# A fused Nystrom attention and squared-ReLU MLP on one core: every batch's steps on three engines follow a written list, and PSUM banks are given out by role

## The chip, the cores and the metric

The kernel runs on one core of a Trainium2 chip. The time is device microseconds of one execution, taken as the median of several. A core has five engines that run side by side, each with its own queue of instructions: TensorE (PE in the profile, with its weight loads as PEld), VectorE (DVE), ScalarE (ACT), GpSimd (POOL) and SyncE (SP). PE writes its results to PSUM, which has eight banks; DVE and ACT read them from there.

## The reference

```python
# q, k, v: 8 batches x 8 heads x 576 rows x 64; m = 32 landmarks
q_lm = q.reshape(B, H, m, S // m, D).mean(axis=3)      # segment means, the same for k
A, Bm, C = sm(q, k_lm), sm(q_lm, k_lm), sm(q_lm, k)    # softmax of 1/8 * a @ b.T
Z = Bm.T / (norm1(Bm) * norminf(Bm) + 1e-06)
for _ in range(6):
    Z = 2 * Z - Z @ Bm @ Z                             # an approximate inverse of Bm
x = (A @ Z @ C @ v)                                    # heads side by side: 4608 x 512
h = x @ w_in                                           # 512 x 2048
out = relu(h) ** 2 @ w_out                             # 2048 x 512, float32
```

## The kernel before

One batch at a time goes through attention and then through the MLP. The attention output x of a batch is never formed. The kernel keeps the transposed A of a batch (the tile `AT`) and multiplies the small rest (Z, C, v) into `w_in`, which gives `G`. Then h is `G` times `AT`.

The attention of a batch is made of these steps, all in `attention`:

- `prepare` casts the loaded k or q (`raw`) to the layout that the matmuls want (`nat`, one DVE copy of 128x2048 each, L189). From batch 3 on (`DMA_T`) it also issues the DMA transposes from SP that make `T` from `nat` and `tT` from the 64 tail rows (L191, L197). Batches 0 to 2 are transposed by PE (`transposed`, L227) and copied out of PSUM by DVE and ACT. `nat` has one buffer for k and one for q, and the raw loads share two.
- `segment_means` (L254, L264), `landmark_scores` (L284) and `landmark_softmax` make the landmark matrix. `inverse_begin` and `inverse_first` prepare its inverse.
- The inverse is a chain: three `joint_step`, one `last_joint_step`, then two pairs of `b_times_v` and `newton_step`. Each is two small matmuls on PE (L326), one or two short DVE operations on their result (L331, L317), and then the next pair of matmuls, which needs what DVE wrote.
- `scores` (L409) and `tails` (L419) multiply `T` and `tT` with the landmarks, and ACT takes the exponential (L413, L421, L424). `a_quad_sums` and `a_rows` normalise A on DVE (L433, L445), `a_transposed` makes `AT` (L455), and `c_values` makes C times v (L477, L483).
- The last part folds: `wt` (L602), its copy (L609), and four groups of matmuls `g` (L627), whose results ACT and DVE copy to `G` in turn (L640 for the first and third, L642 for the second and fourth).

The MLP of a batch has 16 calls of `mlp_in` (four matmuls `h` at L656, a ReLU `r` on ACT at L663, a square to `gT` on DVE at L664) and its output tiles. `mlp_out` makes 16 matmuls for one tile of 128 rows (L686), then ACT copies the tile out of PSUM (`o_sb`, L695) and issues its DMA (L704). Two batches make nine tiles, because the 64 tail rows of both share one.

The work of neighbouring batches is interleaved. While batch b goes through `mlp_in`, batch b + 1 goes through attention, and output tiles of earlier work fill in. The call order comes from the loop at the end of the kernel: three or two output matmuls after each `mlp_in`, and a share of the attention's steps by `attend`. Only batch 0's opening is under `manual_schedule`, where an engine's instructions stand as the code emits them. For all else the framework's scheduler places the instructions of each engine, and some `issue_after` lines hold single ones back.

Loads of k, q and v are issued from POOL in one queue: at the start, `w_in` in four parts, v and k and q of batches 0 and 1, `w_out` in four parts, and then batch 2 and so on, each one when its buffer is free.

PSUM before: `h` has two buffers of two banks each (for `mlp_in`, for `g` and for some output tiles), the tag `n` has three buffers of one bank that everything else takes in turn, output tiles included, and `o` has one bank for the remaining output tiles.

Of the kernel before, what the change touches and what calls it, by code (L numbers as in the profile page):

```python
# [30 lines left out]
DMA_T = 3  # L31


@with_exitstack
def kernel(
# [134 lines left out]
    def ntile(shape, dt=F32):  # L170
        return psum.tile(shape, dt, tag="n", bufs=3, name="n")
# [39 lines left out]
    def attention(b: int, R: dict):  # L211
# [6 lines left out]
        def transposed(nm, half):  # L218
            if not first:
                tps = ntile([P, 2, NPAIR, P], BF16)[:]  # L220
            else:
                if half == 0:
                    X["tps"] = psum.tile([P, 4, NPAIR, P], BF16, tag="h", bufs=2, name="tps")
                tps = X["tps"][:, 2 * half:2 * half + 2, :, :]
# [9 lines left out]
        def transposed_tail():  # L234
            tps = ntile([P, NPAIR, P], BF16)
# [6 lines left out]
        means = ntile([P, 2, NPAIR, M])  # L242
# [36 lines left out]
        def landmark_scores():  # L279
            bm = ntile([P, 2, M])  # L280
# [39 lines left out]
        def products(diagonal, moving):  # L320
            n, w = moving(0).shape[-1], diagonal.shape[-1]
            res = ntile([P, 2, n])
# [11 lines left out]
        def inverse_begin():  # L334
# [3 lines left out]
            if first:  # L338
                rows = ntile([P, 2, M])
# [64 lines left out]
        def scores(nm, qd):  # L404
            sc = ntile([P, NC4, 2, 2, M])
# [10 lines left out]
        def tails():  # L416
            tl = ntile([P, NPAIR, 2, 2 * M])
# [32 lines left out]
        def a_transposed(i):  # L450
            tps = ntile([P, (NC4 + 1) * P], BF16)
# [13 lines left out]
        def c_values():  # L465

            cv = ntile([P, 2, D + 1])
# [67 lines left out]
        else:  # L535
            segment_means(1, "k")
            yield
            if b == 1:
                for half, evac in ((0, dve), (1, act)):
                    evac(*transposed("k", half))  # L540
                    yield
            segment_means(0, "q")
            yield
            landmark_scores()
            landmark_softmax()
            yield
            if b < DMA_T:
                dve(*transposed("q", 0))
            yield
            begun = inverse_begin()  # L550
            yield
            BT, ED = inverse_first(*begun)
            yield
            if b < DMA_T:
                act(*transposed("q", 1))
                yield
                if b > 1:
                    dve(*transposed("k", 0))
                    yield
                    act(*transposed("k", 1))  # L560
                    yield
                transposed_tail()
                yield
            side = [[(scores, "q", 0)], [(scores, "q", 1)], [(tails,)],
                    [(a_quad_sums, 0), (scores, "k", 0)], [(scores, "k", 1), (a_rows, 0)],
                    [(a_quad_sums, 1), (a_transposed, 0)], [(c_values,)],
                    [(a_rows, 1)], [(a_transposed, 1)]]

# [3 lines left out]

        if not first:
            aside()
            yield
        for it in range(3):
            EY, ED, last = joint_step(EY, ED)
            if it == 0 and b > 1:
                X["kpin"] = X["qpin"] = last
# [7 lines left out]
        for it in range(2):  # L587
# [6 lines left out]
            if it == 0 or not first:  # L594
                aside()
            yield
        zt = y.rearrange("p q a m -> p q (a m)")


        wt = ntile([P, 2, P])  # L600
        for qd in range(2):
            nc.tensor.matmul(wt[:, qd, :], lhsT=cvb.rearrange("p q d -> p (q d)"), rhs=zt[:, qd, :],  # L602
                             start=True, stop=True)
        WT = small.tile([P, 2, P], BF16, tag="WT", name="WT")
        if first:
            aside()
            nc.scalar.copy(WT[:], wt[:])
        else:
            last = nc.vector.tensor_copy(WT[:], wt[:])  # L609
        if b == 1:  # L610
            X["kpin"] = last
        if first:
            warm(2)
        yield


        for n in range(4):
            with in_turn() if first and n >= 2 else (
# [13 lines left out]
            if first:  # L632
                for c in ((0, 256), (256, 512)) if n == 0 else ((0, 512),):
                    if c[0]:
                        a_transposed(1)
# [162 lines left out]
```

## Time and profile before

| what | value |
|---|---|
| median of 4 runs | 269.95 us (269.52 to 270.41) |
| the profiled execution | 270.41 us, of which the span from first to last instruction is 268.6 us |
| instructions | PE 2793 matmuls, DVE 492, ACT 278, POOL 70 |
| matmuls of `mlp_in` (L656) and of `mlp_out` (L686) | 512 and 592 |

A page of the profile gives busy time by engine, then the chain of work that ended last, then groups of instructions by source line with busy time, the mean duration of one, and the idle time before them with what ended it. The timeline lists instructions by start time in us, then their length. Matmuls are pipelined: the length of one is from its start until its result is written, and the next one can start long before that. The distance from start to start is therefore what a matmul costs PE. The chip's clock for PE was granted in full throughout.

### The profile page before, as it was taken

Reading aid. Unit: us, or ns where it says so; the run is one execution under the profiler, and the core shown is the slowest. Engines: PE = TensorE matmul, PEld = TensorE weight load, DVE = VectorE, ACT = ScalarE, POOL = GpSimd, SP = SyncE. Lnnn points to the kernel's source line nnn. Section 1 sums busy time; section 2 is a strip of 40 time slices with the busy share of each in tenths; the row PEclk is TensorE's granted clock in tenths of the full one; section 3 lists DMA queues with packets and bytes.
Section 4 is the critical chain, followed back from the end, with each engine's and each line's share of the span. In section 5 each row is a group of like instructions: output and inputs, shape, how many; then the busy total and the mean of one; then the engine's idle time right before and its main releaser. Section 6 shows DMA issues by size and latency. Waiting matters only on the chain.

```text
span 268.6 us, 6785 instructions
## 1 busy us (share of the span) xinstructions
PE 252.2 (94%) x2793; PEld 149.4 (56%) x2793; DVE 175.8 (65%) x492; ACT 158.0 (59%) x278; POOL 46.2 (17%) x70
## 2 busy tenths in 40 slices
PE   2878899999999999999999999999999999999994
PEld 0745565467645665466555665466546665466443
DVE  4686878887965679458955778458945767454000
ACT  2367866369726774468736774478646673587110
POOL 8834333312220121021120132000000000000000
PEclk9999999999999999999999999999999999999999
DMA  8999999999899969992999979991811111210222
GB/s 183 181 205 196 206 203 190 226 189 142 97 162 207 148 124 158 136 180 45 149 171 180 104 133 167 125 158 57 181 41 39 41 39 41 78 43 15 63 81 78
DMA packets 69791, 34.65 MB, mean 129 GB/s; under 512 B 37376, under 2 KB 64256, under 8 KB 69760
## 3 DMA queue, kind: packets, MB, share of 16 engines
q0 software_dynamic: 39808, 17.83, 56.8%
q1 hardware_dynamic: 24704, 7.08, 20.4%
q10 hardware_dynamic: 5248, 9.31, 10.9%
q8 instruction: 22, 0.36, 0.5%
q14 instruction: 9, 0.07, 0.1%
HBM read 36.70 MB, written 9.44 MB: 172 GB/s over the span
## 4 chain that ended last, share of the span: by engine, by line
PE 72%; DVE 8%; ACT 7%; DMA 6%; issue 3%; POOL 2%; POOLq 0%; DVEq 0%; ACTq 0%
PE ops L686 34%; PE h L656 17%; PE n L686 7%; DMA w_out_bf<-in_moe_w_out_dram 6%; ACT G L640 3%; PE g L627 3%; ACT r L663 2%; PE n L254 2%; DVE ra L433 2%; PE n L326 2%; DVE gT L664 2%; PE n L409 2%; PE n L455 1%; PE n L477 1%; PE n L227 1%
## 5 line engine op out<-in xcount | busy, mean ns | idle before, releaser
L686 PE MATMUL ops<-w_out_bf,gT 128*128 128x512 bf16 (+1 forms) x480 | 119.5, 372 | 1.8 <-DMA w_out_bf<-in_moe_w_out_dram 1.3
L663 ACT ACTIVATE r<-h 128x576 bf16<-128x576 f32 x128 | 82.9, 658 | 27.1 <-PE h L656 22.8
L656 PE MATMUL h<-AT,G 128*128 128x288 bf16 x512 | 83.2, 285 | 1.8 <-ACT G L640 1.2
L664 DVE TENSOR_TENSOR gT<-r 128x576 bf16<-128x576 bf16 x128 | 58.0, 454 | 33.4 <-ACT r L663 32.5
L686 PEld LDWEIGHTS <-gT 128*128 128x128 bf16 x592 | 53.4, 97 | 39.9 <-issue 6.9
L656 PEld LDWEIGHTS <-G 128*128 128x128 bf16 x512 | 45.2, 97 | 21.6 <-issue 5.3
L695 ACT COPY o_sb<-ops 128x512 f32<-128x512 f32 (+1 forms) x29 | 16.7, 578 | 35.2 <-PE ops L686 35.2
L686 PE MATMUL n<-w_out_bf,gT 128*128 128x512 bf16 x112 | 31.9, 380 | 0.0
L642 DVE CAST G<-g 128x1024 bf16<-128x1024 f32 x14 | 17.1, 1225 | 13.0 <-PE g L627 12.9
L640 ACT CAST G<-g 128x1024 bf16<-128x1024 f32 x14 | 14.2, 1012 | 11.5 <-PE g L627 11.5
L409 PEld LDWEIGHTS <-T 128*128 128x128 bf16 x256 | 11.3, 98 | 5.4 <-issue 0.3
L326 PEld LDWEIGHTS <-ED 128*128 128x128 bf16 x84 | 7.2, 97 | 11.4 <-DVE ED L317 5.3
L445 DVE TENSOR_TENSOR an<-EA,rra 128x640 bf16<-128x640 f32 (+2 forms) x17 | 13.2, 779 | 0.2
L82 POOL DMA_DIRECT2D qkt<-in_k_dram x8 | 5.8, 720 | 43.9 <-PE n L264 29.3
L433 DVE TENSOR_REDUCE ra<-EA 128x20 f32<-128x640 f32 (+1 forms) x19 | 13.0, 701 | 0.4
L409 PE MATMUL n<-bd,T 128*128 128x64 bf16 x256 | 12.8, 193 | 0.0
L104 POOL DMA_DIRECT2D vm<-in_v_dram x8 | 7.1, 883 | 33.0 <-PE n L477 31.4
L459 ACT COPY AT<-n 128x576 bf16<-128x576 bf16 x9 | 5.8, 640 | 11.8 <-PE n L455 11.8
L94 POOL DMA_DIRECT2D raw<-in_k_dram x7 | 6.7, 959 | 29.5 <-DVE nat L189 18.8
L254 PEld LDWEIGHTS <-nat 128*128 128x128 bf16 x256 | 8.9, 97 | 5.0 <-DVE gT L664 1.4
L413 ACT ACTIVATE EA<-n 128x512 f32<-128x512 f32 x16 | 9.5, 600 | 2.2 <-PE n L409 2.1
L413 ACT ACTIVATE EC<-n 128x512 bf16<-128x512 f32 x16 | 9.6, 603 | 1.2 <-PE n L409 0.7
(125 smaller groups left out, 268.4 us busy)
## 6 DMA issues: line engine op xcount, KB each, us to landing
out_dram<-o_sb ACTq DMA_DIRECT2D x31, 256.0 KB, 4.3
vm<-in_v_dram POOLq DMA_DIRECT2D x8, 512.0 KB, 14.3
raw<-in_k_dram POOLq DMA_DIRECT2D x7, 512.0 KB, 10.3
raw<-in_q_dram POOLq DMA_DIRECT2D x7, 512.0 KB, 14.8
w_in_bf<-in_moe_w_in_dram POOLq DMA_DIRECT2D x4, 512.0 KB, 11.4
w_out_bf<-in_moe_w_out_dram POOLq DMA_DIRECT2D x4, 512.0 KB, 16.0
out_dram<-o_sb ACTq DMA_DIRECT2D x9, 128.0 KB, 2.4
raw<-in_k_dram SPq DMA_DIRECT2D x1, 1024.0 KB, 5.4
```

The costliest lines, as they stand in the source:

```text
L254: nc.tensor.matmul(means[:, ti, p, :], lhsT=src.rearrange("p h d -> p (h d)"), rhs=seg[:, c + (ti if c == NC4 else 0), :], start=(n == 0 a ...
L409: nc.tensor.matmul(sc[:, c, j, :, :], lhsT=X[nm + "T"][:, c, p, :], rhs=BD[:, 1 if nm == "q" else 0, p, 0:64], start=True, stop=True)
L413: nc.scalar.activation((EA if nm == "q" else EC)[:, qd, 0:NC4, :], sc.rearrange("p c j i m -> p c (j i m)"), AF.Exp, scale=SCALE)
L433: nc.vector.reduce_sum(ra[:, quads, lo:hi, :], EA[:, quads, lo:hi, :].rearrange("p q c (h m) -> p q c h m", m=M), axis=AX.X)
L445: nc.vector.tensor_tensor(an[:, i, lo:hi, :].rearrange("p c (h m) -> p c h m", m=M), EA[:, i, lo:hi, :].rearrange("p c (h m) -> p c h m", ...
L640: nc.scalar.copy(dst, gg[:])
L642: last = nc.vector.tensor_copy(dst, gg[:])
L656: last = nc.tensor.matmul(h[:, j, 0:HALF], lhsT=G[:, qd, f * P:(f + 1) * P], rhs=AT[:, qd, j * HALF:(j + 1) * HALF], start=(qd == 0), stop ...
L663: nc.scalar.activation(r.rearrange("p (j t) -> p j t", j=2), h[:, :, 0:HALF], AF.Relu)
L664: return nc.vector.tensor_tensor(gT[:, f, o:o + S], r[:], r[:], ALU.mult)
L686: mark[:] = [nc.tensor.matmul(ops, lhsT=gT[:, f, t * P:t * P + P], rhs=w_out_bf[:, f, i * n:i * n + n], start=(f == 0), stop=(f == NF - 1))]
L695: nc.scalar.copy(o_h, ops)
```

## The change

All batches now run under `manual_schedule` for PE, DVE and ACT, so that the instructions of each of these engines stand in the order in which the code emits them. That order is read from a list for each batch (`PLANS`): batch 0, batch 1, then one list for even and one for odd batches, and one for the last. POOL and SP are still placed by the scheduler.

In a list `h` is one `mlp_in` of batch b up to its ReLU, and `s` is the square of the oldest `h` that has none yet, so that DVE's square can stand apart from its ReLU. A number is so many matmuls of the output tiles. The other words are attention steps of batch b + 1: `mk` and `mq` are the segment means, `lm` and `ls` the landmark scores and their softmax, `ib` and `if` the start of the inverse, `jo` and `jl` the joint steps, `nu` and `nn` the later pairs, `sq0` to `sk1` the scores, `tl` the tails, `as` and `ar` the sums and rows of A, `at` its transposition, `cv` the C values, `wt` the fold, and `gg0` and `gg1` two of the four groups `g` each. `tk`, `tq` and `tt` are PE transposes, in the first two lists only. `pk` and `pq` are `prepare`, and a `+` means one batch further.

PSUM: `h` serves `mlp_in` and `g` alone. `n0` holds the attention's results, one at a time; `n1` holds the products of the inverse, the transposes of q, and the fold; `n2` and `o` take output tiles in turn. While batch 0's own attention runs, the three `n` banks are still taken in turn.

The output DMA of a tile is issued from ACT after the third matmul of the next tile instead of straight after its copy, other than in the last batch.

```diff
+PLACED = 1
+BATCH0 = (
+    "h h s s g h pk s h s h h g s h s h s tk0 h h s pq mk s h s h mq tq0 h s s 2 lm ls s h "
+    "tk1 ib tq1 1 h h 1 tt 1 if 2 s 1 sq0 1 jo s 2 sq1 jo s 1 tl jo 2 as0 3 sk1 jl 3 ar0 3 "
+    "sk0 2 as1 1 nu at0 2 ar1 nn pk+ 1 cv 1 nu nn1 1 at1 wt pq+ 2 gg0 2 gg1"
+)
+BATCH1 = (
+    "1 mk 1 h tq0 1 h mq h s tq1 2 lm h s 1 s h ls 1 tt s 1 s h ib sq0 h s 2 h tl 1 if 4 s "
+    "sq1 as0 2 jo h tk0 s 1 h jo 1 s tk1 1 pk+ 1 h jo s pq+ 1 sk0 1 as1 3 sk1 1 jl ar0 s h 1 "
+    "h ar1 cv 1 nu h 1 s h nn at0 3 nu 1 s 1 h nn1 3 s 1 wt at1 2 s 2 s 1 gg0 8 gg1 12"
+)
+EVEN = (
+    "2 h h 2 s s 1 mk mq 1 h 1 s 3 lm h ls 1 sq0 h 1 s 1 h 1 s ib 3 s tl h 2 if sq1 h as1 3 "
+    "jo sk0 h pk+ 2 s as0 2 s 2 jo s 1 h sk1 h 2 s h pq+ jo cv 2 jl s 1 ar0 2 h h 1 s nu 1 "
+    "ar1 2 h nn s 1 s h at0 s 3 nu 3 at1 1 nn1 4 wt s 4 gg0 5 gg1 7"
+)
+ODD = (
+    "2 h s mk 1 h 1 h mq 1 h 2 lm 1 s ls 1 s h s 4 s sq0 1 ib h 1 s tl if 2 h 1 sq1 h pk+ 1 "
+    "jo s as0 s 1 h 1 sk0 2 s 1 h 1 sk1 jo 1 s 1 h as1 h jo s pq+ 1 cv jl 4 h s ar0 1 nu h "
+    "ar1 3 s 1 nn h 3 s at0 h 1 nu at1 1 s 1 nn1 3 s 3 wt 4 gg0 8 gg1 15"
+)
+LAST = (
+    "1 h h 1 s 4 h 1 s s h 1 h 2 s 1 h 1 s 6 s 1 h s h 3 h s 2 h 1 s 2 s 1 h 2 s 3 h 2 s h h "
+    "1 s 3 h 4 h 7 s s s"
+)
+PLANS = [BATCH0, BATCH1, EVEN, ODD, EVEN, ODD, EVEN, LAST]
...
-    def ntile(shape, dt=F32):
-        return psum.tile(shape, dt, tag="n", bufs=3, name="n")
+    turn = [0]
+
+    def ntile(shape, dt=F32, place=0, placed=True):
+        if not placed:
+            place = turn[0] = (turn[0] + 1) % 3
+        return psum.tile(shape, dt, tag="n%d" % place, bufs=1, name="n%d" % place)
...
-                tps = ntile([P, 2, NPAIR, P], BF16)[:]
+                tps = ntile([P, 2, NPAIR, P], BF16, place=int(nm == "q"), placed=b >= PLACED)[:]
...
-            res = ntile([P, 2, n])
+            res = ntile([P, 2, n], place=1, placed=b >= PLACED)
...
+        def folded_c(zt):
+            wt = ntile([P, 2, P], place=1, placed=b >= PLACED)
+            for qd in range(2):
+                nc.tensor.matmul(wt[:, qd, :], lhsT=cvb.rearrange("p q d -> p (q d)"),
+                                 rhs=zt[:, qd, :], start=True, stop=True)
+            return wt, small.tile([P, 2, P], BF16, tag="WT", name="WT")
+
+        def step(name):
+            st = X["state"]
+            kind, i = name[:2], int(name[2:] or 0)
+            if kind == "mk":
+                segment_means(1, "k")
+            elif kind == "mq":
+                segment_means(0, "q")
+            elif kind in ("tk", "tq"):
+                (dve, act)[i](*transposed(kind[1], i))
+            elif kind == "tt":
+                transposed_tail()
+            elif kind == "lm":
+                landmark_scores()
+            elif kind == "ls":
+                landmark_softmax()
+            elif kind == "ib":
+                st["begun"] = inverse_begin()
+            elif kind == "if":
+                st["BT"], st["ED"] = inverse_first(*st["begun"])
+                st["EY"] = EY
+            elif kind in ("sq", "sk"):
+                scores(kind[1], i)
+            elif kind == "tl":
+                tails()
+            elif kind == "as":
+                a_quad_sums(i)
+            elif kind == "ar":
+                a_rows(i)
+            elif kind == "at":
+                a_transposed(i)
+            elif kind == "cv":
+                c_values()
+            elif kind == "jo":
+                st["EY"], st["ED"], last = joint_step(st["EY"], st["ED"])
+            elif kind == "jl":
+                st["y"], st["v"] = last_joint_step(st["EY"], st["ED"])
+            elif kind == "nu":
+                st["UD"] = b_times_v(st["BT"], st["v"])
+            elif kind == "nn":
+                st["y"], st["v"], last = newton_step(st["y"], st["UD"], i == 1)
+            elif kind == "wt":
+                wt, st["WT"] = folded_c(st["y"].rearrange("p q a m -> p q (a m)"))
+                last = nc.vector.tensor_copy(st["WT"][:], wt[:])
+                if b == 1:
+                    X["kpin"] = last
+            elif kind == "gg":
+                for n in (2 * i, 2 * i + 1):
+                    if True:
+                        gg = psum.tile([P, 2, 512], F32, tag="h", bufs=2, name="g")
+                        g_of(st["WT"], [gg[:, e, :] for e in range(2)], n)
+                    last = (act, dve)[n % 2](G[:, :, n * 512:n * 512 + 512], gg[:])
+                if b == 1:
+                    X["qpin"] = last
+                if i == 1:
+                    R[b] = (AT, G)
+            else:
+                assert False, name
+
+        def g_of(WT, g, n):
...
-        return nc.vector.tensor_tensor(gT[:, f, o:o + S], r[:], r[:], ALU.mult)
+        return lambda: nc.vector.tensor_tensor(gT[:, f, o:o + S], r[:], r[:], ALU.mult)
+
+    leaving = []
+
+    def leave():
+        while leaving:
+            leaving.pop(0)()
...
-            elif (t % NC4 == 0 and not first and t < 8 or (b, t) == (0, 1)
-                  or b == B - 1 and t % 2 == 0):
-                halves = [psum.tile([P, 2, DM], F32, tag="h", bufs=2, name="ops2")[:, 0, :]]
-            elif t % NC4 == 2 and b < B - 1:
-                halves = [ntile([P, DM])[:]]
+            elif (b // 2 + t) % 2:
+                halves = [ntile([P, DM], place=2)[:]]
...
+                    if f == 2:
+                        leave()
...
-                    queue.dma_start(rows[:, c, i * n:i * n + n], o_h)
+                    leaving.append(partial(queue.dma_start, rows[:, c, i * n:i * n + n], o_h))
+                if b == B - 1:
+                    leave()
...
-        early = [0, 0, 0, 0, 0, 0, 1, 2, 3, 3, 4, 5, 7, 9, 12, half]
...
-            advance(tiles, 3 if b % 2 == 0 else 2)
-            attend(early[f] if b == 0 else (f + 1) * half // NF)
...
+    def outputs():
+        for b in range(B):
+            yield from mlp_out(b, gTs[b // 2])
+    def follow(b, plan):
+        AT, G = R.pop(b)
+        f, squares = 0, []
+        for token in plan.split():
+            n = b + 1 + token.count("+")
+            name = token.rstrip("+")
+            if name == "h":
+                squares.append(mlp_in(b, f, AT, G, gTs[b // 2]))
+                f += 1
+            elif name == "s":
+                squares.pop(0)()
+            elif name.isdigit():
+                advance(outs, int(name))
+            elif name == "g":
+                advance(start, 1)
+            elif n >= B:
+                pass
+            elif name in ("pk", "pq"):
+                prepare(n, (name[1],))
+            else:
+                step_of(n)(name)
+        assert f == NF and not squares, (b, f, squares)
+    outs = outputs()
+    with tc.manual_schedule(engines={mybir.EngineType.PE, mybir.EngineType.DVE,
+                                     mybir.EngineType.Activation}):
+        for b in range(B):
+            load_next()
+            if b % 2 == 0:
+                gTs[b // 2] = mlp.tile([P, NF, 2 * S], BF16, tag="gT", name="gT")
+            follow(b, PLANS[b])
+        for _ in outs:
+            pass
```

## The prediction

> **What bounds the kernel now.** I read the page first, then the busy time by stage, then the timelines of PE and DVE where stages meet, then single transfers.
>
> ```profile
> span 268.6 us, 6785 instructions
> PE 252.2 (94%) x2793; PEld 149.4 (56%) x2793; DVE 175.8 (65%) x492; ACT 158.0 (59%) x278; POOL 46.2 (17%) x70
> ...
> PE 72%; DVE 8%; ACT 7%; DMA 6%; issue 3%; POOL 2%; POOLq 0%; DVEq 0%; ACTq 0%
> ```
>
> PE is busy for 94% and carries 72% of the chain that ended last. By stage (stretch, its length, busy us of PE, PEld, DVE, ACT and POOL, granted clock, DMA share, GB/s):
>
> ```profile
> 24.00:36.00 12.00, 10.32 (x122) 7.00 (x121) 8.82 (x19) 9.99 (x20) 4.67 (x6) 1.00 1.34 202
> 36.00:54.70 18.70, 18.32 (x244) 9.85 (x243) 16.05 (x49) 10.55 (x19) 6.53 (x9) 1.00 1.51 205
> 54.70:83.00 28.30, 28.16 (x331) 17.37 (x330) 22.74 (x63) 19.41 (x34) 5.32 (x7) 1.00 1.18 154
> 83.00:114.70 31.70, 31.06 (x333) 18.10 (x333) 21.66 (x60) 18.95 (x33) 4.72 (x6) 1.00 1.21 148
> ```
>
> From 24 us on PE hardly stands still. But busy time hides waits under about 0.2 us, since a matmul lasts longer than its start-to-start distance. So I price PE by that distance:
>
> ```profile
> 90.22 0.65 PE L656 MATMUL h<-AT,G 128*128 128x288 bf16 x4
> 90.71 0.81 PE L686 MATMUL ops<-w_out_bf,gT 128*128 128x512 bf16 x3
> 91.36 0.20 PE L326 MATMUL n<-btc,BT 128*128 128x32 bf16 x2
> 91.41 0.65 PE L656 MATMUL h<-AT,G 128*128 128x288 bf16 x4
> 91.90 0.81 PE L686 MATMUL ops<-w_out_bf,gT 128*128 128x512 bf16 x3
> 92.54 0.40 PE L409 MATMUL n<-bd,T 128*128 128x64 bf16 x8
> ```
>
> Four `h` cost 0.49 us, an output matmul 0.216, a product pair 0.05, a score group 0.23. Read off in the same way, the attention of a batch is means 0.91, landmarks 0.10, four scores 0.92, tails 0.22, products 0.5, `at` 0.56, `cv` 0.69, `wt` 0.11, `gg` 1.3: 5.3 us. Two batches are 2 x 5.3 + 32 x 0.49 + 144 x 0.216 = 57.4 us. From the first `h` of batch 4 (142.94) to that of batch 6 (202.60) it took 59.66. So about 2.3 us of waits per two batches is all that a better order can win there, and in the first batch some 4 us.
>
> **The change, part by part.** The matmuls, copies and loads are the same; only order and banks change. So I walked each list: PE's own sum by the distances above, and DVE and ACT behind it. On DVE a square takes a slot of 0.38 us, a cast 0.62, a row sum 0.74 and its reciprocal 0.2 to 0.3, a joint step 0.5; on ACT a ReLU takes 0.55, an exponential 0.49, `o_sb` 0.47. A result crosses engines in 0.2 to 0.25 us.
>
> *Batch 0's list is held by loads.* The list has 35 output matmuls; before, 45 were done when batch 1's first `h` began at 54.71. The old order at that point is
>
> ```profile
> 51.42 0.68 DVE L189 COPY nat<-raw 128x2048 bf16<-128x2048 bf16 x1
> 52.32 1.22 DVE L642 CAST G<-g 128x1024 bf16<-128x1024 f32 x1 [0.21 <-PE g L627]
> 53.46 0.68 DVE L189 COPY nat<-raw 128x2048 bf16<-128x2048 bf16 x1
> 54.24 1.23 DVE L642 CAST G<-g 128x1024 bf16<-128x1024 f32 x1
> ```
>
> The cast of q (53.46) stands behind a `G` copy. In the list `pq+` comes before both `G` copies. Its raw q was loaded so:
>
> ```profile
> L94 POOL DMA_DIRECT2D raw<-in_q_dram x1: 881/881/881, 37.0 to 37.0; - x1
> ...
> DMA to landing us min/median/max: 14.8/14.8/14.8
> ```
>
> It landed at 51.8, and POOL's queue up to it is unchanged. Then come the cast 0.68, the `G` copy 1.22 that frees an `h` buffer, and half of `gg1`, 0.35: the list ends at 54.1. If q lands 0.8 sooner (the second output tile is stored later), the DVE chain (`nn1`, `zt`, `wt`, cast, copy) ends it at 53.3. I take 53.7. By then PE has waited for DVE's joint steps and casts. The wait for `w_out` (1.3 us in the list of PE's waits) goes, since 13 `h` precede its first use, but that gain ends in the same wait. Batch 1's first `h` comes at about 54.5 with 36 output matmuls done: nine fewer (1.9 us), 0.2 earlier: **+1.7 us**. Bounds: +1.2 to +2.2. Rule beside row: the Trainium skill (Perfetto Trace Analysis, Tensor Engine Instruction) calls DVE and ACT strict first in, first out, which speaks against a cast with an open load ahead of `G`. By the rule nothing passes the cast; if the copy could pass, the list would end about 0.6 sooner (+1.1). The DVE waits of before show a cast holding it 2.7 us for raw k, so I keep +1.7.
>
> *Batch 1's list.* PE's sum is 29.1; single waits add 1.4 (`sq0` behind the `tT` copy 0.26 and `sq1` behind the two tail exponentials 0.28, both on bank `n0`; `nn` 0.75 behind sums and rows on DVE). The old order did the same work in 28.32 + 6 x 0.216 + 0.40 = 30.0. **+0.5**.
>
> *Even and odd lists.* In an even list (times from its start) PE does `sq1` at 9.06. ACT, behind two tail exponentials and a ReLU, has its exponential at 9.63 to 10.23. On DVE `as1` follows to 11.24, the first joint step to 11.76, `pk+` to 12.38, a square, `as0` to 13.78, a square, the second joint step 14.16 to 14.68, two squares, `pq+` to 16.06, and the third joint step, whose result is there at 16.7. PE has done everything ahead of `jl` by 16.2 and waits 0.5; with `gg1`'s second half behind DVE's `G` copy 0.2 and others 0.2 the sum of 27.9 becomes 28.8. Old, for 80 - 12 output matmuls: 31.38 - 2.59 = 28.8. **0**. Odd: `as1` holds the third joint step to 15.35 (PE is there at 15.0), and `pq+` and `cv`'s scaling hold `nu`: 29.6 plus 0.4, 0.2 and 0.2 is 30.4 against 28.28 + 2.59 = 30.9. **-0.5** each. The even list of batch 6 has no casts: **-0.6**. Last list and rest: **-0.3**.
>
> *Transposes.* Now the scores come early: `sq0` at 5.4 us of an even list, where before they stood 9.5 us after the first `h` (92.54 against 83.03). They need `T` of q. Batch 3's pair:
>
> ```profile
> L191 SPq DMA_TRANSPOSE T<-nat x2: 2272/5870/9469, 68.7 to 71.0; - x2
> ...
> DMA to landing us min/median/max: 11.7/15.9/20.1
> ```
>
> So q's landed at 91.1. With the casts at 14.2 and 16.3 of batch 1's list they start when they did before (68.7, about 70), on a DMA system as full (its slices read 9), with `tT` of batch 4 now ahead of them on SP, which is no later than its tail loads (landed at 68.1 before). PE reaches `sq0` at 53.7 + 30.5 + 5.4 = 89.6, and the landing, too, comes 0.2 sooner with the list: **+1.3** (0 to 3). All that is behind it on PE waits. For batches 4 and 6, casts 4 us apart, landing 18 to 23 us after k's cast meets a need after 22.5: 0 to 0.5, I take 0. Rule beside row: the Trainium skill (DMA: Bandwidth & Descriptors, Latency and other measured facts) gives a DMA transpose 261 GB/s; 0.5 MB would take 2 us, an estimate, and this +1.3 would be 0. The row has 20.1, and the last pair, with no loads beside it, still took 7.5 for q. I take the row.
>
> *Banks and stores.* Output tiles no longer take `h` buffers: PE's waits show `h` after ACT `r` once, 0.4 us, so 0 to -0.4, in the sums above. One bank for the attention costs the `n0` waits named. A later store issue saves ACT nothing: an issue lasts 0.33 us but the next ReLU had started before it. If that cover went, each issue would cost up to that.
>
> Sum, batches in order: 1.7 + 0.5 + (0 + 1.3) - 0.5 + 0 - 0.5 - 0.6 - 0.3 = **+1.6**. Against the profiled execution (span 268.6, 270.41 in all) that is 272.0; that execution lies 0.46 above the median of the runs, 269.95, so the forecast is 271.5 us.
>
> **The rivals.**
> *DVE keeps up (faster).* One mechanism: DVE's queue between `sq1` and `jl`. If `as1` can start when PE's scores are there (9.3, not 10.2), or DVE's slots are a tenth shorter than I took them, DVE has caught up by the third joint step. The point is 0.5 us there. Then the waits of the walk are gone: 1.0 of batch 1's 1.4, 0.7 in two even lists, 0.6 in two odd ones: 1.6 - 1.0 - 1.4 - 1.2 = -2.0, 267.9 us; without the transpose wait 266.6. For it: DVE is busy 65% only. Against: in the old order, too, PE waited 2.3 us per two batches, and the chain of the inverse passes DVE nine times per batch, now in a fixed order.
> *The lists only trade waits (no change).* The same chain, cast and transposes bind in both; batch 0's loss is won back by 0.3 us in each later list: 270.
> *Transposes decide (far slower).* If q's `T` lands 21.1 us after its own issue, as batch 5's did (128.8 to 149.9), batch 1's list leads to a wait of 1.6 and two even lists to 2.4 in the next odd one (issue 16.2, need 34.9): 1.6 + 0.3 + 4.8 = +6.7, 276.6 us. It decides from 18.7 us after issue. Against: q's is issued 4 us after k's there, so less of k's is still ahead of it.
>
> **How the numbers follow.** Forecast 0.45, no change 0.18, DVE keeps up 0.27, transposes 0.10. Faster means below 269.15 and slower above 270.75 (0.3%, about what a measurement of this kernel can tell from no change): faster 0.27, same 0.18, slower 0.55. The forecast's own range is 270.5 to 273. The range of 266.8 to 274.0 reaches over the gain with and nearly without the transpose wait, and into the start of the transpose case.
>
> **What would show it.** Right: batch 1's first `h` at 54 to 55 with 36 output matmuls done; DVE's `nat` copy for q before its first `G` of that list; PE idle at batch 3's first scores (L440) until a transpose lands; batch 4 to batch 6 in about 59.2 us. Wrong: 45 output matmuls by 54.7, or batch 4 to batch 6 in less than 58.3, or no wait of PE on joint steps.

## The result and the profile after

The changed kernel takes 269.5 us (median of 43 runs, 268.2 to 270.97), the kernel before, beside it, 269.85 (64 runs): a ratio of 0.9976, 95% interval 0.9965 to 0.9986. Measured again with later runs (e11) it stood at 0.9972, 0.9944 to 1.0. So it is faster by a quarter of a per cent; the forecast was 271.5, slower.

The page of the changed kernel (its profiled execution took 268.94 us; before's took 270.41):

```profile
span 267.2 us, 6791 instructions
PE 250.1 (94%) x2793; PEld 150.3 (56%) x2793; DVE 177.3 (66%) x492; ACT 157.1 (59%) x278; POOL 45.6 (17%) x70
...
PE 56%; DVE 21%; DMA 15%; ACT 4%; issue 3%; ACTq 0%
```

The chain has more of DVE and of loads than before: in batch 0's list PE now waits for both. By stage (stretch, length, busy us of PE, PEld, DVE, ACT and POOL, granted clock, DMA share, GB/s), cut at the first `h` of batches 1, 2, 3 and 4:

```profile
36.00:54.64 18.64, 16.19 (x230) 9.15 (x229) 16.20 (x48) 10.53 (x17) 7.58 (x9) 1.00 1.51 198
54.64:84.51 29.87, 29.24 (x337) 17.97 (x336) 23.43 (x63) 20.07 (x34) 4.70 (x6) 1.00 1.23 168
84.51:112.91 28.40, 28.18 (x322) 16.96 (x320) 21.32 (x59) 17.99 (x32) 4.69 (x6) 1.00 1.06 141
112.91:143.32 30.41, 29.99 (x330) 17.54 (x328) 21.24 (x59) 18.62 (x33) 4.71 (x6) 1.00 1.17 166
```

PE does 2 us less in the first stretch than before, and hardly stands still in the others. To compare lists that do different numbers of output matmuls, I take the first `h` of each batch and the output matmuls done by then (PE's matmuls, counted in the trace) and charge 0.216 us for each one fewer. The column "behind" is how far the changed kernel lags the old one; its steps stand against the prediction's.

| up to | before | after | behind | step | predicted step |
|---|---|---|---|---|---|
| batch 1's `h` | 54.71, 45 done | 54.64, 37 | +1.66 | +1.66 | +1.7 |
| batch 2's | 83.03, 103 | 84.51, 101 | +1.91 | +0.25 | +0.5 |
| batch 3's | 114.66, 183 | 112.91, 169 | +1.27 | -0.64 | 0, and +1.3 for the transpose |
| batch 4's | 142.94, 247 | 143.32, 245 | +0.81 | -0.46 | -0.5 |
| batch 5's | 174.32, 327 | 171.72, 313 | +0.42 | -0.39 | 0 |
| batch 6's | 202.60, 391 | 201.85, 389 | -0.32 | -0.74 | -0.5 |
| batch 7's | 233.98, 471 | 229.63, 456 | -1.11 | -0.79 | -0.6 |
| last matmul | 264.69 | 263.30 | -1.39 | -0.28 | -0.3 |

(The transpose is awaited in batch 2's list, at batch 3's scores.) Sum: -1.39 where +1.6 was forecast. Between the same two `h` both kernels run the same matmuls other than output matmuls, so the steps compare like with like. Batch 0's end is as forecast, in place and size. DVE's timeline at that end:

```profile
50.55 0.42 DVE L620 CAST WT<-n 128x256 bf16<-128x256 f32 x1 [0.38 <-PE n L574]
51.57 0.69 DVE L220 COPY nat<-raw 128x2048 bf16<-128x2048 bf16 x1 [0.60 <-DMA raw<-in_q_dram]
52.18 1.22 DVE L628 CAST G<-g 128x1024 bf16<-128x1024 f32 x1
53.93 1.22 DVE L628 CAST G<-g 128x1024 bf16<-128x1024 f32 x1 [0.53 <-PE g L639]
```

The cast of q stands idle for its load and the `G` copy starts the moment it ends. PE, behind it, has its waits here:

```profile
49.37 0.21 PE L357 MATMUL n<-y,ED 128*128 128x32 bf16 x2 [1.14 <-DVE ED L348]
...
52.57 0.41 PE L639 MATMUL g<-w_in_bf,WT 64*32 64x512 bf16 x8 [0.38 <-ACT G L628]
53.45 0.41 PE L639 MATMUL g<-w_in_bf,WT 64*32 64x512 bf16 x8 [0.47 <-DVE G L628]
```

The forecast wait for q's transpose isn't there. PE's timeline at batch 3's first scores, and the transposes' queue (an answer for line 222 between 70 and 71.5 us):

```profile
89.22 0.38 PE L732 MATMUL ops<-w_out_bf,gT 128*128 128x512 bf16 x1
89.43 0.40 PE L440 MATMUL n<-bd,T 128*128 128x64 bf16 x8
```

```profile
L222 SPq DMA_TRANSPOSE T<-nat x2: 2122/5243/8364, 68.5 to 70.8; - x2
...
DMA to landing us min/median/max: 7.5/13.1/18.6
```

Issued at 70.76, landed at 89.38; PE came at 89.43. It fits by 0.05 us, which is luck: when the same kernel was profiled again (e11), PE waited 0.39 us there. Before, the pair took 11.7 and 20.1 us; now 7.5 and 18.6.

### The profile page after: what moved, and what is told of

The parts are those of the page before. It is cut to its first block, busy times and chain, and to the rows that moved or that the text cites. A ratio compares the mean times of both kernels' runs of the same rounds, so it can differ in the third digit from the quotient of the medians.

```text
span 267.2 us, 6791 instructions
## 1 busy us (share of the span) xinstructions
PE 250.1 (94%) x2793; PEld 150.3 (56%) x2793; DVE 177.3 (66%) x492; ACT 157.1 (59%) x278; POOL 45.6 (17%) x70
## 4 chain that ended last, share of the span: by engine, by line
PE 56%; DVE 21%; DMA 15%; ACT 4%; issue 3%; ACTq 0%
PE ops L732 18%; PE n L732 16%; PE h L700 13%; DMA raw<-in_k_dram 7%; DMA raw<-in_q_dram 5%; DVE gT L708 5%; DVE ra L464 3%; PE g L639 3%; DVE nat L220 2%; DMA w_in_bf<-in_moe_w_in_dram 2%; ACT r L707 2%; PE n L285 2%; DVE ED L348 1%; PE n L486 1%; DVE EY L362 1%
## 5 line engine op out<-in xcount | busy, mean ns | idle before, releaser
L707 ACT ACTIVATE r<-h 128x576 bf16<-128x576 f32 x128 | 81.5, 656 | 41.3 <-PE h L700 30.3
L700 PE MATMUL h<-AT,G 128*128 128x288 bf16 x512 | 81.2, 286 | 0.9 <-ACT r L707 0.8
L732 PE MATMUL ops<-w_out_bf,gT 128*128 128x512 bf16 (+1 forms) x320 | 81.5, 368 | 0.0
L708 DVE TENSOR_TENSOR gT<-r 128x576 bf16<-128x576 bf16 x128 | 55.6, 446 | 31.8 <-ACT r L707 30.9
L732 PE MATMUL n<-w_out_bf,gT 128*128 128x512 bf16 x272 | 72.4, 379 | 0.0
L700 PEld LDWEIGHTS <-G 128*128 128x128 bf16 x512 | 47.4, 97 | 22.9 <-issue 1.8
L743 ACT COPY o_sb<-ops 128x512 f32<-128x512 f32 (+1 forms) x19 | 10.9, 576 | 12.4 <-PE ops L732 12.1
L743 ACT COPY o_sb<-n 128x512 f32<-128x512 f32 x17 | 10.0, 586 | 10.9 <-PE n L732 10.3
L109 POOL DMA_DIRECT2D qkt<-in_k_dram x8 | 5.7, 709 | 53.8 <-PE n L295 42.6
L440 PE MATMUL n<-bd,T 128*128 128x64 bf16 x256 | 12.7, 193 | 0.1
L220 DVE COPY nat<-raw 128x2048 bf16<-128x2048 bf16 x14 | 10.1, 720 | 1.3 <-DMA raw<-in_k_dram 0.7
L639 PE MATMUL g<-w_in_bf,WT 64*32 64x512 bf16 x232 | 9.4, 383 | 1.0 <-DVE G L628 0.5
```

The lines of the kernel that those rows point to most:

```text
L220: nc.vector.tensor_copy(X[nm][:], raw)
L440: nc.tensor.matmul(sc[:, c, j, :, :], lhsT=X[nm + "T"][:, c, p, :], rhs=BD[:, 1 if nm == "q" else 0, p, 0:64], start=True, stop=True)
L639: nc.tensor.matmul(g[i][M * p:M * p + M, :], lhsT=WT[64 * i:64 * i + 64, i, M * p:M * p + M], rhs=w_in_bf[64 * i:64 * i + 64, p, n * 512:n ...
L700: last = nc.tensor.matmul(h[:, j, 0:HALF], lhsT=G[:, qd, f * P:(f + 1) * P], rhs=AT[:, qd, j * HALF:(j + 1) * HALF], start=(qd == 0), stop ...
L707: nc.scalar.activation(r.rearrange("p (j t) -> p j t", j=2), h[:, :, 0:HALF], AF.Relu)
L708: return lambda: nc.vector.tensor_tensor(gT[:, f, o:o + S], r[:], r[:], ALU.mult)
```

## The experiments

Each changes the lists of the changed kernel, unless said. "List n" is the time from batch n's first `h` to the next batch's. The changed kernel's lists 1 to 6 take 29.87, 28.40, 30.41, 28.40, 30.13 and 27.78 us; a list that an experiment doesn't touch repeats within 0.02, which makes single profiles good to that in these places. List 2 is the exception, since it holds the wait for q's transpose: 28.80 in e11. A wait in brackets is the profile's idle time; the waits that I give for `jl`, `nu`, `nn` and e11's scores are taken from start-to-start distances, as in the prediction, and are longer by about 0.15.

**e1: fewer output matmuls at the turn.**

```
-BATCH1 ... 1 gg0 8 gg1 12     +... 7 gg0 11 gg1 3
-EVEN   ... 4 gg0 5 gg1 7      +... 6 gg0 7 gg1 3
-ODD    ... 4 gg0 8 gg1 15     +... 10 gg0 14 gg1 3
```

> In the lists of batches 1 to 6, the output matmuls that follow gg1 are cut to 3 (as many as stood there before the change); the 4 to 12 others go ahead of gg0 and between gg0 and gg1. The same matmuls are done in each list. Theory (the gain of the later lists is the cover at the batch turn: 7 to 15 output matmuls after gg1, so that the next h finds its banks copied out): each of the six turns gets back a wait of PE on a G copy of 0.3 to 0.6 us, as the old order had it at each turn: +2 to +3.5 us against the changed kernel, about 271.5 to 273. Rival (the gain is that DVE's and ACT's steps stand at better places inside the lists): the turns cost under 0.1 us each, total +0 to +0.6.

Measured 269.98 us, ratio to before 0.9982 (0.9954 to 1.0011). Lists: 29.97, 28.38, 30.42, 28.39, 30.15, 27.88. Only 0.2 us is lost in sum, as the rival has it. But with the one or two output matmuls ahead of the next `h`, 4 or 5 still lay in the turn.

**e5: as many as before the change.** As e1, with `gg1 1`, so that 2 or 3 are left.

> As e1, but only 1 output matmul is left behind gg1 in the lists of batches 1 to 6, so that with the 1 or 2 at the start of the next list 2 or 3 lie between gg1 and the next h (before the change 3; in e1 4 or 5; in the changed kernel 8 to 17). Theory (the old order lost its 0.33 us at every turn, because 3 output matmuls, 0.65 us, don't cover ACT's G copy of about 1 us, while 4 or 5 do): each of six turns gets a wait of PE at h of 0.3 to 0.5 us, +1.8 to +3 us against the changed kernel, near 271.3. Rival (the turn has nothing to do with it): each list within 0.1 us of the changed kernel's.

Measured 271.49 us, ratio 1.0049 (1.0031 to 1.0067); lists 30.28, 28.71, 30.74, 28.71, 30.47, 28.30: +0.3 to +0.5 in each of the six, +2.2 in sum. PE's waits (engine, tile and line; total us, times, longest) in the old kernel, and then in this one:

```profile
PE h L656 <- ACT G L640: 1.2, 6, 0.4
```

```profile
PE h L700 <- ACT G L628: 1.2, 6, 0.4
```

The same wait, six times, comes back with the old number of output matmuls, and the changed kernel has no such row. So the theory of e1 was right with another threshold. From the start of the last `g` matmul to the next `h` it takes 1.3 us in five of the old kernel's turns (1.55 in one) and in all of e5's, with 3 output matmuls or 2. With 5 it takes 1.41, their own time (e1); with 4 it is 1.29, and a wait of 0.1 is left (e1's list 6). More add nothing. The turn, 2.2 us, is most of what the lists of batches 1 to 6 win (their steps sum to 2.77). e5 has the new banks, so the banks alone don't give it; the old order with the new banks was not tried.

What these lists still lose shows in PE's waits from batch 3's `h` to batch 6's, before the change and after it:

```profile
PE h L656 <- ACT G L640: 0.8, 3, 0.4
```

```profile
PE n L357 <- DVE ED L348: 0.5, 3, 0.2
PE n L357 <- DVE v L406: 0.3, 1, 0.3
```

The turn's waits have gone; waits for the inverse's steps on DVE have come.

**e3: q's cast and transpose later.** In BATCH1 `pq+` moves from behind the third `jo` to ahead of `ar1`.

> In batch 1's list the cast of batch 3's q (pq+), and with it q's transpose on SP, is moved about 3.3 us later (from behind the third joint step to ahead of ar1). Nothing else moves. In the changed kernel the transpose landed 18.6 us after its issue at 70.8, at 89.4, just as PE reached batch 3's first scores. Theory A (the transpose takes a set time from its issue): it lands at 92.6 and PE waits 2.5 to 3.2 us there: +2.5 to +3 us. Theory B (the loads that share the DMA engines set the landing, and the transpose goes through when they are done): it lands within 1 us of 89.4, +0 to +1 us.

Measured 269.26 us, ratio 0.9961 (0.9942 to 0.998). The transpose was issued 1.8 us later (72.58; the cast, behind others on DVE, moved less than I had expected of PE's list) and landed at 89.81, 0.43 later. List 1 29.72, list 2 28.91. Theory B: this transpose's landing is not a set time behind its issue.

**e7: both casts together.** In BATCH1 `tk1 1 pk+ pq+ 1 h jo s 1 sk0`.

> In batch 1's list pq+ is put directly behind pk+, as DVE had both casts before the change; q's cast, its transpose's issue and the next raw q load all come about 0.9 us earlier. Theory (the load of raw q that the cast sets free shares the DMA engines with k's transpose: in the old order it started 1.1 us after k's transpose was issued and that took 11.7 us, in the changed kernel 1.9 us after and it took 7.5): k's transpose takes about 12 us, q's lands at 90 to 91.5 although it is issued earlier, and PE waits 0.8 to 2 us at batch 3's first scores: +0.8 to +2 us in the list of batch 2. Rival (a transpose lands a set time after its issue): it lands at about 88.5, no wait, 0.

Measured 269.87 us, ratio 0.9984 (0.9968 to 1.0001); list 2 29.88, +1.48. The transposes, and PE at batch 3's scores:

```profile
DMA to landing us min/median/max: 11.3/15.4/19.5
```

```profile
91.17 0.41 PE L440 MATMUL n<-bd,T 128*128 128x64 bf16 x8 [1.30 <-DMA T<-nat]
```

The theory holds: k's transpose takes 11.3 us, where it took 11.7 before the change, and q's lands at 91.12, as before. The next raw loads, which the casts set free, started so before the change, in the changed kernel and here (k's transpose was issued at 68.66, 68.53 and 69.15):

```profile
68.86 0.89 POOL L94 DMA_DIRECT2D raw<-in_k_dram  x1 [2.27 <-DVE nat L189]
69.74 0.89 POOL L94 DMA_DIRECT2D raw<-in_q_dram  x1
```

```profile
68.73 0.89 POOL L121 DMA_DIRECT2D raw<-in_k_dram  x1 [7.00 <-DVE EY L362]
70.40 0.88 POOL L121 DMA_DIRECT2D raw<-in_q_dram  x1 [0.79 <-DVE nat L220]
```

```profile
69.16 0.88 POOL L121 DMA_DIRECT2D raw<-in_k_dram  x1 [7.01 <-DVE nat L220]
70.04 0.89 POOL L121 DMA_DIRECT2D raw<-in_q_dram  x1
```

So raw q's load came 1.1, 1.9 and 0.9 us behind k's transpose. Raw k's came 0.20, 0.20 and 0.01 behind, so e7 alone doesn't tell the two loads apart; with the old kernel, where raw k's distance is that of the changed one, it is raw q's that goes with the slow transpose. One joint step and one square between the casts are worth 1.3 us on PE.

**e12: less traffic.** Of batch 4's raw q one head of eight is loaded.

> As the changed kernel, but of batch 4's raw q only one head of eight is loaded; POOL clears the other seven in SBUF (so batch 4's result is that of a q with zeros there). Its 512 KB load was under way from 70.4 to 83.0 us, beside q's transpose for batch 3, which in eight runs landed at 89.1 to 89.8 us whether it was issued at 70.5 or at 72.6 us, as did the load of v that was issued behind it. Theory (the DMA engines work through all that is queued by 73 us, and the transpose is done when the queue is): with 448 KB less of about 2.5 MB it lands 1.5 to 3 us sooner, at 86.5 to 88, and PE never waits at batch 3's first scores: list of batch 2 at 28.40 us. Rival (the transpose's own pace sets it, about 13 us behind k's transpose): it lands at 89.0 to 89.8 again. Either way the time changes by 0 to -0.4 us, since PE comes there at 89.2 to 89.4.

Measured 269.49 us, ratio 0.9974 (0.9956 to 0.9993). The transposes:

```profile
L225 SPq DMA_TRANSPOSE T<-nat x2: 2156/4862/7567, 68.0 to 70.2; - x2
...
DMA to landing us min/median/max: 8.1/12.2/16.3
```

q's landed at 86.57 instead of 89.38, 2.8 us sooner where the theory expects 1.5 to 3, and list 2 is 28.40. So the landing depends on what is queued on the DMA engines with it. With the same loads, and k's transpose at 7.5 to 8.7 us, it came at 88.9 to 90.1 in ten profiles, e6 among them, where the loads began 1.1 us later; but at 91.1 and 91.0 in e4 and e8, where they began 1.3 to 1.6 later. How the landing follows from the issue times is not worked out.

**e2: batch 0's waits filled.** Seven output matmuls more in batch 0's list, seven fewer in batch 1's.

```
-BATCH0 ... 1 nu nn1 ... 2 gg0 2 gg1       +... 1 nu 4 nn1 ... 2 gg0 5 gg1
-BATCH1 ... tk1 1 pk+ ... as1 3 sk1 ... at1 2 s 2 s 1 gg0
+BATCH1 ... tk1 pk+ ... as1 1 sk1 ... at1 s s 1 gg0
```

> Seven output matmuls more in batch 0's list, where PE waited: 4 between nu and nn1, 3 more between gg0 and gg1; seven fewer in batch 1's list (1 ahead of pk+, 2 behind as1, 4 behind at1). Theory (batch 0's loss is PE standing still while raw q, its cast and the G copies set the end of the list): the seven fit into waits of 1.29 and 0.54 us, the first h of batch 1 comes at the same 54.6 us with 44 instead of 37 outputs done, and the whole is 7 x 0.216 = 1.5 us less than the changed kernel (0.9 to 1.5, as batch 1's list has less to cover its own waits). Rival (the waits only move: PE's later arrival at gg1 pushes the G copies, or batch 1's list stands still for what it no longer covers): 0 to -0.4.

Measured 271.44 us, ratio 1.0037 (1.001 to 1.0064): slower than both kernels. Batch 1's first `h` came at 54.51 with 44 outputs done, so 1.6 us were won there, as the theory has it. List 1 then took 30.34 for seven outputs fewer, 2.0 more than its share: outputs now followed their squares too closely (PE waited 1.0 for `gT`), and at k's scores PE lost 0.7. And list 2 took 30.64:

```profile
91.99 0.41 PE L440 MATMUL n<-bd,T 128*128 128x64 bf16 x8 [2.06 <-DMA T<-nat]
```

The transpose landed at 91.95: the next raw k load started 0.1 us ahead of k's transpose here (0.2 behind it in the changed kernel), raw q's 1.6 behind (1.9), and k's took 12.7 us. So the rival was right about the end, and more so than it said.

**e8: q's cast last in batch 0's list.** `wt 2 gg0 2 gg1 pq+`.

> In batch 0's list pq+ (the cast that waits for raw q of batch 2, landed at 51.5) moves from ahead of gg0 to behind gg1; the G copies no longer stand behind it on DVE. Theory (the cast's place sets the end of batch 0's list: in all runs so far the first h of batch 1 comes 3.1 us after the landing of raw q): DVE's first G copy goes 0.8 to 1 us sooner and batch 1's first h at about 53.8 instead of 54.6, with the same 37 outputs; -0.8. Of this 0.5 to 0.8 is lost again at batch 3's first scores, where q's transpose landed just in time, if its landing doesn't move with it: -0.8 to 0 in all. Rival (PE has its own reasons to end there, DVE's chain from nn1 on): 54.4 to 54.6, 0.

Measured 269.49 us, ratio 0.999 (0.9976 to 1.0004). From the `WT` cast to batch 1's first `h` it took 3.64 us (51.64 to 55.28) where the changed kernel took 4.09: the cast's place costs 0.45, not 0.8; the other 3.64 us, with four `G` copies through two `h` buffers, stay without it. The times themselves lie later than forecast (`h` at 55.28 for 53.8) since this profile's batch 0 ran 1.1 us late up to the `WT` cast. List 1 then took 30.58, as its first transposes wait 0.52 for that cast. Nothing won.

**e4: two banks in turn instead of roles.**

```
+        elif place < 2:
+            place = turn[0] = (turn[0] + 1) % 2
```

> From batch 1 on, every result of the attention takes the two banks n0 and n1 in turn, as it comes, instead of n1 for the inverse's products, wt and q's transposes and n0 for all else; output tiles keep n2 and o. Order of the instructions unchanged. Theory (the split by role keeps the short products of the inverse out of the way of the long exponentials; that is part of the gain): PE waits for ACT's exponentials at joint steps, +0.5 to +2 us. Rival (order alone is the gain, banks hardly matter): within 0.3 us, or up to 0.5 us less, since sq1 no longer waits for the exponential of sq0 or of the tails in bank n0.

Measured 270.52 us, ratio 1.0019 (0.9998 to 1.0041). List 1 30.16 (+0.29) and list 2 28.58 (+0.18, of it 0.16 at the scores that wait for the transpose), lists 3 to 6 as they were. Batch 0's end was 1.3 later, but there the clock was at half (below). The roles of `n0` and `n1` are worth 0.3 us: the rival, at its bound.

**e6: output tiles in the old banks.** The choice of bank in `mlp_out` as before.

> The output tiles take the banks that they took before the change (every fourth an h buffer, others n2 and o) while the order stays that of the lists. Theory (a part of the gain is that an output tile no longer takes one of the two h buffers, and finds its own bank copied out): the old order's waits at the start of an output tile, 0.26 us twice in batches 4 and 5, come back, and h waits for the one buffer left: +0.5 us per list, +3 us in all. Rival (the lists put enough work between two h): within 0.5 us in all.

Measured 278.58 us, ratio 1.0324 (1.0302 to 1.0346); each list 1.3 to 1.8 longer. PE's longest waits:

```profile
PE g L639 <- ACT G L628: 7.0, 7, 1.1
```

`g` waits here for ACT's `G` copy, as an output tile sat in one of the two `h` buffers while `gg0` needed both. It shows that this order can't do without the new banks. It doesn't show what they are worth by themselves, since the old order never put `g` there.

**e9: q's cast behind `jl`** in EVEN (`jo cv 2 jl pq+ s`) and ODD (`1 cv jl pq+ 4 h`).

> In the lists EVEN and ODD the cast pq+ moves from just ahead of DVE's last joint step to behind jl; nothing else moves. In the changed kernel PE waited 0.38 us at jl in the two even lists that have casts, and 0.29 at jl plus 0.15 to 0.43 at nu in the two odd ones. Theory (a 0.6 us cast at the head of DVE's queue is what PE waits for there, as the prediction's walk had it, in size 0.5 and 0.2): these waits go, -0.3 to -0.4 us in each of batches 2 and 4, -0.4 in each of 3 and 5: -1.2 to -1.6 us against the changed kernel. Rival (the cast is then late for something else: nu's result stands behind it, or q's transpose, issued 1 us later, is awaited): 0 to -0.4.

Measured 269.17 us, ratio 0.9958 (0.9929 to 0.9986). Lists 2 to 5: 28.15, 30.34, 28.28, 30.33, in sum 0.24 less. The wait at `jl` in the even lists is gone, and comes back at `nn` (0.23 in list 4), where `nu`'s result now stands behind the cast; in the odd lists `jl` still waits 0.29. The rival.

**e10: all of these at once; e11: the changed kernel again.** e10 has e9's casts, e2's filling with batch 1's `h` drawn forward, and five output matmuls ahead of `sq0` in batch 2's list.

> e9, and: 7 more output matmuls in the waits of batch 0's list (as in e2); batch 1's list with its h drawn forward, so that the 7 fewer output matmuls in it leave the order of squares and outputs whole, pq+ behind jl and two outputs ahead of nn; batch 2's own list holds its sq0 back by 5 output matmuls (1.1 us), taken from around gg0 and gg1, so that PE doesn't reach it before q's transpose has landed. Theory: -1.5 (batch 0) and -1.2 to -1.6 (e9) and up to -0.5 (nn): -2.5 to -3.5 us against the changed kernel, if the transpose lands by 89.5. Rival (batch 0's gain is lost to the transpose, as in e2): the landing stays at 90 to 92 and takes back 0.5 to 2 of it: -0.5 to -2.

> The changed kernel as it is, on the same chip as the two others: a base for them, and a second profile of it. All theories: each list as long as in the first profile within 0.1 us, except where the landing of a transfer decides (the list of batch 0, up to 1 us; batch 3's first scores, where k's transpose takes 7 to 8 us or about 12).

e10 269.33 us, ratio 0.9964 (0.9932 to 0.9996); e11 269.65, ratio 0.9972 (0.9944 to 1.0). In e10 batch 0's filling is won again (batch 1's `h` at 54.52 with 44 outputs), but list 1 gives 1.0 of it back: it takes 29.33 where seven outputs fewer should make 28.36, with 0.97 us of waiting at `nn` instead of 0.71 and 0.4 at k's first scores. Batch 2's `h` comes at 83.85, 0.66 ahead. List 2 takes 28.99: the outputs taken from around `gg0` and `gg1` left PE waiting 0.28 for a `G` copy and 0.24 for the last square. e11 repeats every list within 0.02 but list 2, 28.80: it began at 84.25, the transpose landed at 89.52 as ever, and PE waited 0.39.

**e13: the waits of batch 0's list filled with idle matmuls; e14: e10 with a load held back.** e13 puts five matmuls on zeros between `nu` and `nn1` and three ahead of `gg1`. e14 has batch 2's list EVEN again and v of batch 4 issued after batch 5's tail loads.

> The changed kernel, with 5 matmuls on a block of zeros (result unused, in a free bank) between nu and nn1 and 3 more between gg0 and gg1 of batch 0's list, in the waits of 1.29 and 0.54 us. Theory (PE half idle from 48 to 54 us is what makes the clock halve for 3.4 us in a part of the executions): executions with a mean granted clock under 0.99 fall from 20 in 56 to 1 or 2 in 12, and the median comes 0.3 to 0.6 us lower than the changed kernel's, about 269.1. Rival (the half-clock stretches have nothing to do with these waits, or come from the waits ahead of batch 0's first h): the share stays at about a third, the median at 269.5 or, as the fill delays PE at nn1 and gg1, up to 0.3 higher.

> As e10, but batch 2 keeps the list EVEN (with the cast behind jl) and batch 4's load of v is issued behind the tail loads of batch 5 (near 87 us) instead of at 72 us, beside q's transpose of batch 3. Theory (the transpose is done when the queued traffic is, as e12 showed): with 576 KB less ahead it lands at 86 to 87.5, PE, which comes to batch 3's first scores at about 88.8, doesn't wait, the list of batch 2 takes 28.15 as in e9, and what batch 0's fill wins stays: 268.94 - 1.5 - 0.5 - 0.2 = about 267 us in an undisturbed execution, median 267 to 268. Rival (the late v holds batch 4's c values, needed near 98.5 us, or moves the next transposes): 0.5 to 2 us are lost there, 268.5 to 269.5.

e13 269.42 us, ratio 0.9984 (0.9956 to 1.0013), where its rival had the median; e14 269.74, ratio 0.9984 (0.9965 to 1.0003). In e14 a load of v was still issued at 71.94, ahead of raw q: POOL's queue isn't written by hand, and the edit didn't hold it. The transpose landed at 90.09, PE waited 1.0, list 2 took 29.37. So the held load was not tried. On the clock, see below. No version was shown to be faster than the changed kernel.

## Why the prediction was wrong

Between +1.6 and -1.39 lie 3.0 us. The transpose wait that didn't come makes 1.3 of them, the lists of batches 2 and 4 1.0, batch 1's 0.25, those of batches 5 and 6 0.4. Without the transpose wait the sum would have said no change (+0.3); it takes the even lists as well to turn its sign.

- **Batch 0's list (+1.7): right**, +1.66, with 37 output matmuls where 36 were forecast and the end at 54.64 where 54.5 was. e2 shows that this loss is PE standing still, since seven more output matmuls fit without moving the end. Of the two causes named, the cast with an open load ahead of the `G` copies is worth 0.45 (e8); the wait for DVE's part of the inverse, 1.14 us at `nn1`, is the larger, and e2 put four output matmuls into it.
- **The transpose wait (+1.3): the step that failed.** I took the landing from the row of before (20.1 us after issue) and argued that the DMA system was as full, so q's transpose would land as late. The bytes were the same; their order wasn't. With the casts 1.5 us apart instead of 0.6, the next raw q load started 1.9 instead of 1.1 us behind k's transpose, which then took 7.5 instead of 11.7 us, and q's landed at 89.4 (e7 turns it back). I had placed the casts 2.1 us apart myself and drew nothing from it. Why a load that starts 0.8 us later costs the transpose so much less stays open. The wait is 0 in one profile and 0.39 in the other. The Trainium skill's rate for a DMA transpose (DMA: Bandwidth & Descriptors, Latency and other measured facts), which I set aside, would have made this term 0, which is nearer, but for a wrong reason: the transpose took 18.6 us, not 2.
- **The even lists (0): mis-sized.** Of the 0.9 of waits that I added to PE's own 27.9, `jl` measured 0.38 (0.5 forecast), and of the 0.4 for `gg1` and "others" 0.1 was there: list 28.40, not 28.8. For batch 2 there is 0.25 more: its old list took 31.63, and I compared with the 31.38 of batches 4 and 6.
- **Batch 1's list (+0.5): half of it.** `nn` waited 0.71 (0.75 forecast), the two scores 0.20 and 0.21 (0.26 and 0.28). Two errors of the sum cancel in part: PE's own work was 28.75, not 29.1, and the 0.40 added to the old list stands for no matmul, since the two lists differ by the six outputs alone.
- **Odd lists, batch 6 and the end: right** in sign and within 0.25. The list of batch 3 took 30.41 where 30.4 was worked out. Batch 4 to batch 6 took 58.5 us, between the 59.2 that I named as the sign of being right and the 58.3 of being wrong.
- **What the sum didn't see.** The gain was already inside the old lists' lengths that I compared with, so it needed no name to be counted. But of the old kernel's waits at `h` I named the row "`h` after ACT `r`", once and 0.4 us, and passed over "`h` after ACT `G`", six times and 1.2 us, which is where the change's main gain lies.
- **The rivals.** "DVE keeps up" gave a faster kernel by the wrong road: PE still waits for joint steps. "Transposes decide" was right about where the limit lies, wrong about its side: the transpose came in just under it. It takes back what is won ahead of it (2.06 us in e2, 1.0 in e14, 0.39 in e11). That, and what batch 1's list lost (2.0 in e2, 1.0 in e10), is why filling batch 0's waits didn't pay.

## What to carry to other kernels

Work out a written order's gain at the seams: count what covers the longest copy where one stage hands its buffers to the next (here 3 matmuls were too few and 5 were enough), and look for that wait by name in the old kernel's list. A transfer's landing time is not a property of the transfer: before it goes into a sum, ask what else the same edit puts on the DMA engines beside it, and in which order. Before mending a wait, look for the next fixed time downstream: a gain ahead of it is lost there.

## What the hardware showed

The two profiled executions, both at a granted clock of 1.000, differ by 1.5 us, the medians by 0.35 to 0.74. In 47 of 56 executions of the changed kernel and 55 of 125 of the one before, the mean granted clock is under 0.995. In the profiles with such a clock TensorE ran at half clock for 3.4 us, once or twice, around batch 0's first `h` or near the end of its list. The stretches of e9 from 48 to 54 us (clock third from the right) and a row of PE in it:

```profile
48.00:49.00 1.00, 0.45 (x3) 0.11 (x2) 0.97 (x4) 0.00 (x0) 1.00 (x1) 1.00 1.21 284
49.00:50.00 1.00, 0.46 (x7) 0.34 (x8) 0.69 (x3) 0.00 (x0) 1.00 (x2) 1.00 1.46 196
50.00:51.00 1.00, 0.86 (x8) 0.43 (x6) 0.48 (x3) 0.64 (x1) 0.80 (x2) 0.68 1.46 195
51.00:52.00 1.00, 1.00 (x18) 0.15 (x16) 0.92 (x2) 0.59 (x1) 0.00 (x0) 0.50 1.47 197
52.00:53.00 1.00, 1.00 (x18) 0.13 (x2) 0.32 (x2) 0.72 (x1) 0.68 (x1) 0.50 2.02 167
53.00:54.00 1.00, 1.00 (x16) 0.14 (x15) 0.93 (x1) 0.29 (x1) 0.20 (x1) 0.61 1.94 166
```

```profile
51.57 1.05 PE L639 MATMUL g<-w_in_bf,WT 64*32 64x512 bf16 x16
```

The clock missing from the last four rows is 0.32 + 0.50 + 0.50 + 0.39 = 1.71 us, at half clock 3.4 us; the 16 `g` matmuls take 1.05 us where they took 0.63. In the changed kernel PE is busy for 3.79 of the 6 us from 48 to 54, before it was for 5.83. The Trainium skill (TensorE: Matmul & The Clock Gate, Part 1: The HAM clock gate) tells of half rate after an idle window of about 3.4 us. The length agrees; the cause only in part, since PE was never idle for more than 1.1 us at a time here, and was busy for 2.2 of the 3.4 us ahead of it. The changed kernel's own profile has a stretch with no more (2.05 of 3.4 us, from 47.65) and kept the full clock.

Counted over executions by mean granted clock (one such stretch gives about 0.994, two about 0.987; the middle class also holds 16 and 2 executions at 0.997 or 0.998, which in e13's profile comes from the last microsecond alone):

| | at least 0.9985 | 0.99 to 0.9985 | under 0.99 |
|---|---|---|---|
| before (125) | 54, median 269.88 | 63, 270.21 | 8, 272.17 |
| changed (56) | 7, 268.92 | 29, 269.06 | 20, 270.06 |

Within a class the changed kernel is 1.0 to 2.1 us faster; it falls into the third class more often (20 of 56 against 8 of 125), and that hides a part of the gain. Where the second stretch lies is not settled: e9 has one from 50.4 to 53.8 us besides the one from 23.1 to 26.5, e4 one from 51.7 to 55.1 alone, and e6 and e8 a double one from about 21.7 to 28.5, around batch 0's first `h`. Filling batch 0's waits left 1 of 12 executions under 0.99 in e13, but 6 of 12 in e14, so the waits at 48 to 54 us as its cause stay argued, not shown.
